# Full sections of 24 slots and three units' values, and one held bank for the value sums, in a fused Fourier-mix and attention kernel

## The chip, the cores and the metric

The kernel runs on one core of a Trainium2 chip. The metric is the device time of one execution in microseconds (us), as the median of several runs. The engines are PE (TensorE: matmuls; PEld is its weight loads), DVE (VectorE), ACT (ScalarE), POOL (GpSimd) and SP, which here only issues DMAs. PE writes its results into PSUM, which has eight banks of 128 x 512 floats; DVE and ACT read them from there.

## What is computed

The reference, cut to what matters (S = 2048 rows, D = 512, 32 heads of 16):

```python
g = sigmoid((x * gate_w).sum(-1, keepdims=True))
a = x @ dft_hid_re.T                 # DFT along the hidden axis
b = x @ dft_hid_im.T
y = dft_seq_re @ a - dft_seq_im @ b  # DFT along the sequence, real part
q, k, v = heads(x @ wqkv)
p = softmax(q @ k.T * 16 ** -0.5)    # 32 heads, 2048 x 2048
o = merge(p @ v) @ wo
out = g * y + (1 - g) * o
```

## The kernel before, in words

**Units.** Attention works on 16 pairs of heads. A pair is cut into 32 units: two halves of the queries (1024 each) times 16 tiles of 128 keys. A unit has four score products (two blocks of 512 queries, two heads), each a product of 64 rows with a 128 x 512 result, whose exponential ACT writes into a tile `pt`. Softmax needs the maximum of every query row first, so a second set of products ("maxima", L258) computes the scores the other way round some 70 tiles ahead, and DVE reduces each of those 128 x 512 tiles (L260). So a unit also needs four maxima products. The exact sums of the float32 DFT and projections are made of three products of rounded parts each (`ch`/`cl` are the two parts of a chunk of the DFT matrix).

**Sections.** PE's order is written out by patterns of slots. A slot of a section issues one product of a DFT or projection chain (L473) on one half of the 128 rows, and beside it one score (`s`, L797) or maxima (`a`, L258) product on the other half; the two run side by side. A section ends with `|`: there the planned loads are issued, and then the values of two units, products of `pt` with `vt` (L833), which use all 128 rows and 32 columns each, four beside each other. Sections come in pairs: the same chain products run first with rows 0 to 63 (half 0; the scores are those of head 1), then with rows 64 to 127 (half 1; the scores are those of head 0). Head 0 starts two units ahead, so that each section can end with the values of two units of both heads.

**Stages.** After the first projections, 12 pairs of THIN sections carry the real part of the hidden DFT, 96 pairs of FULL sections the DFT along the sequence, one EVEN and 15 TEN pairs the output projection; the last 16 units have a tail of their own. A FULL section has 16 slots, 8 of each kind. A chunk of the DFT matrix is 12 products; POOL splits it into two parts (`c_split`, L418 and L419) three chunks ahead, and SP loads it four chunks ahead (`c_load`). A whole sum over the sequence takes four chunks, 48 products; then ACT copies it out scaled (L527, L530).

**Banks.** One of the eight banks, `psD`, belongs to the chain. The other seven are handed out by `bank()`, a small planner that keeps for each bank the time at which it expects its reader to be done, and takes the one that comes free first. Which bank a product gets is thereby fixed when the program is built. Scores and maxima take banks, and so did each section's values: `pv` took one, ACT copied it to `oe` (L842), and POOL added it to `osum` (L848) in the next section. The first copy of each sixteen units goes straight to `osum` (L839).

**Order between halves.** The first chain product of a section waits for a reader of the section before: the exponential of its last score product (`tc.add_manual_dep` in `segment`).

**Buffers.** `pt` has four buffers of four 512-column blocks, one per unit. A buffer is handed out again when all that read it are done; the first exponential into it waits for that.

Of the kernel before, what the change touches and what calls it, by code (L numbers as in the profile page):

```python
# [13 lines left out]
ALU = mybir.AluOpType  # L14
# [18 lines left out]
def mix_kernel(ctx: ExitStack, tc: tile.TileContext, xa_t, xa, wqkv, w_hid, w_seq, wo, gate_w, out):  # L33
# [487 lines left out]
    def dft_next(c, tt, s, t, chain, yr):  # L521
        if c == 0 and tt == NT - 1:
            nc.sync.dma_start(t.bitcast(F32), b_d[s])
        if s == NT - 1:
            y = work.tile([P, D], F32, name="y", bufs=2)
            if c == 0:
                nc.scalar.activation(y, chain.ps, AF.Copy, scale=g[:, tt:tt + 1])  # L527
# [12 lines left out]
        if s % 4 == 3:  # L540
            i = (c * NT + tt) * 4 + s // 4
            c_split(i + 3)
            c_load(i + 4)


# [110 lines left out]
    def finish(ps, t, y, other=False, n=1):  # L656
        if other:

            for c in range(n):
                cols = slice(c * D // n, (c + 1) * D // n)  # L660
                tmp = few[0][:, t % 4, cols]
# [104 lines left out]
    last_pairs = []  # L766

    def last_pair(fill):
        few.append(work.tile([P, 4, D], F32, name="few", tag="pt", bufs=4))
# [13 lines left out]
    def scores(u, qb, h, ps=None):  # L783
        p, r = divmod(u, 32)
        hf, kt = divmod(r, 16)
        q0 = hf * 1024 + qb * 512
        if u >= UNITS - 16:

            blk, kt = divmod(kt, 8)
            q0, kt = 1024 + blk * 512, 2 * kt + qb  # L790
        if u not in pts:
            pts[u] = work.tile([P, 4, 512], F32, name="pt", bufs=4)
        if ps is None:
            i, ps = bank()
            read_by(i, "s")
        rr = slice(64 * h, 64 * h + 64)
        nc.tensor.matmul(ps, ks[p % 2][rr, kt * P:(kt + 1) * P], qs[p % 2][rr, q0:q0 + 512], start=True, stop=True)  # L797
        return nc.scalar.activation(pts[u][:, 2 * qb + h], ps, AF.Exp, bias=0.0, scale=DH ** -0.5)  # L798

    held = []  # L800

    def pv_last(u):
        nonlocal now
        blk, k2 = divmod(u - UNITS + 16, 8)
        pt = pts.pop(u)
        if k2 == 0:
            i, acc = bank()
            free[i] = 1e9
            held[:] = [i]
            last_pairs.append(LastPair(blk, acc))  # L810
        acc = last_pairs[-1].acc
        for j in range(4):
            x, h = divmod(j, 2)
            nc.tensor.matmul(acc[32 * j:32 * j + 32], vt[:, 2 * k2 + x, NP - 1, h:h + 32], pt[:, j],  # L814
                             start=k2 == 0, stop=k2 == 7)
        now += 3.75
        if blk == 0 and k2 == 7:
            last_pairs[0].copy(1)
            free[held[0]] = now + 6

    osum = work.tile([P, 2, 512], F32, name="osum", tag="w15")

    def pv(us):

        nonlocal now
        i, acc = bank()
        for u in us:
            p, r = divmod(u, 32)
            hf, kt = divmod(r, 16)
            pt = pts.pop(u)  # L830
            for j in range(4):
                h = j % 2
                nc.tensor.matmul(acc[32 * j:32 * j + 32], vt[:, kt, p, h:h + 32], pt[:, j],  # L833
                                 start=u == us[0], stop=u == us[-1])
        now += 3.75 * len(us) + 1
        read_by(i, "s")
        o = osum[:, hf]
        if kt + 1 == len(us):
            nc.scalar.copy(o, acc)  # L839
            return  # L840
        oe = work.tile([P, 512], F32, name="oe", bufs=2)
        nc.scalar.copy(oe, acc)  # L842
        adds.append(partial(add_sum, o, oe, p, hf, kt == NT - 1))

    adds = []

    def add_sum(o, oe, p, hf, whole):
        nc.gpsimd.tensor_tensor(o, o, oe, ALU.add)  # L848
        if whole:
            for qb in range(2):  # L850
                nc.sync.dma_start(o_d[hf][p, :, qb * 512:(qb + 1) * 512], o[64 * qb:64 * qb + 64])

    def add_sums():
        while adds:
            adds.pop(0)()

    def take(gen, n, whole=True):

# [37 lines left out]
    for p in range(2, NP):  # L896
        u = 32 * (p - 1)
        at(u - 18, load_q, p, LOW)
        for kb in range(4):
            cols = slice(kb * 512, (kb + 1) * 512)  # L900
            if 2 < p < NP - 1:
                at(u - 16 + 4 * kb, load_rows, p, 1, cols, (1,))
                at(u - 14 + 4 * kb, load_rows, p, 1, cols, (0,))
            else:
                at(u - 14 + 4 * kb, load_rows, p, 1, cols)
        at(u - 2, load_q, p, HIGH)

    for hf in range(2):
# [28 lines left out]

    FULL = "a s a s a s a s s a s a s a a s |"  # L940
    THIN = "aS s a s a s s a s a s a a sA |"
    EVEN = "aA s s a s ^ s d s sA a d sS |", "a s a sS a ^ s a s s s s a |"
    TEN = "aA s s a s ^ s s s a a sS |", "a s a sS a ^ s s s s s aA |"
# [19 lines left out]
            else:  # L963
                users.append((kind, scores(*x)))

    def values():
        nonlocal valued
        us = valued, valued + 1
        valued += 2
        if us[0] < UNITS - 16:  # L970
            pv(us)
        else:
            for u in us:
                pv_last(u)

    def segment(pattern, half, ds, stop, between=None, hold=True):


        nonlocal now
        nonlocal users  # L980
        before, users = users, []
        ds, late = iter(ds), []
        back = late if hold else None
        for n, slot in enumerate(pattern.split()):
            if slot == "|":
                for f in late:
                    f()
                add_sums()
                run_plan(valued)
                if between:  # L990
                    between()
                values()
                continue
            if slot == "^":
                if deferred:
                    deferred.pop(0)()
                continue
            now += 1
            ahead = n and len(slot) == 1 and slot != "d" and pattern in (THIN, *TEN)
            if ahead:  # L1000
                score(slot[0], 1 - half)
            if len(slot) == 1:
                x = next(ds, None)
                if x:

                    before = before if x[0].begun else None
                    i = issue(x, half, stop, back)
                    users = []
                    if before:
                        tc.add_manual_dep(  # L1010
                            i.ins, dict(before[::-1]).get("s", before[0][1]).ins.name,
                            mybir.DependencyInfo(mybir.DependencyClass.Sync, mybir.DependencyReason.DATA))
                        before = None
            if not ahead and slot != "d":
                score(slot[0], 1 - half)
            if len(slot) == 2:
                score(slot[1].lower(), half)
        if deferred:
            deferred.pop(0)()

    def pairs():

        for i in range(NT - 4):
            yield (THIN,) * 2, take(hid, 12)
        for i in range(2 * NT * 3):
            yield (FULL,) * 2, take(seq, 16)
        for patterns, n in ((EVEN, 1), (TEN, 15)):
            for i in range(n):
                yield patterns, take(both_first, 9)
# [14 lines left out]
    def first_tiles(phase, j):  # L1044
# [16 lines left out]
    def in_between():  # L1061
# [49 lines left out]
```

## Time and profile before

| | |
|---|---|
| time, median of 3 runs | 1651.18 us (1650.62 to 1653.74) |
| profiled execution, first to last instruction | 1649.2 us |
| PE busy | 1641.4 us, clock granted in full |
| DVE busy | 1356.8 us |
| ACT busy | 1268.2 us |
| POOL busy | 754.5 us |

The page gives no time of its own for the profiled execution beside its span; the runs were timed apart from it. In the profile's rows, `L473` is a line of the kernel, `d<-xab,ch` the tile written and those read, `x16` a number of instructions, and in a timeline the first two columns are the start and the length in us. A bracket at the end is idle time before the instruction and what ended it. In the rows by group, the numbers behind the bar are the busy time in us, the mean length of one in ns, and the idle time ahead with what ended most of it. In the rows by window, the busy time of PE, PEld, DVE, ACT and POOL follow the window's length, and the granted clock stands before the share of the DMA engines. A value product of float32 is recorded as two matmuls.

### The profile page before, as it was taken

The numbers are of one execution on the slowest core, as the hardware profiler recorded it, in microseconds if no ns is written. First come the engines' busy times: TensorE is split into PE (matmuls) and PEld (weight loads), VectorE is DVE, ScalarE is ACT, GpSimd is POOL, SyncE is SP. The second block draws the span as 40 slices with busy tenths as digits, with TensorE's granted clock in tenths as the row PEclk, the third lists the DMA queues.
The fourth block names the chain that finished last, engine by engine and source line by source line (L and its number), as shares of the span: only waits on it lengthen the run. The fifth ranks groups of instructions, "written<-read, shape, count | busy, mean of one in ns | idle before, by whom it ended". The sixth has DMA issues, their size and how long they took to land.

```text
span 1649.2 us, 35245 instructions
## 1 busy us (share of the span) xinstructions
PE 1641.4 (100%) x13169; PEld 1017.0 (62%) x13169; DVE 1356.8 (82%) x2285; ACT 1268.2 (77%) x2487; POOL 754.5 (46%) x813
## 2 busy tenths in 40 slices
PE   9999999999999999999999999999999999999998
PEld 7888855556656666566665666666666556655544
DVE  5469988888888888888888888888888888877776
ACT  5312188888888888888888888887888888899996
POOL 0224643554544555545454565554545566332341
PEclk9999999999999999999999999999999999999999
DMA  9953301112221224222227334322222233451024
GB/s 291 353 161 135 155 14 38 29 53 66 67 72 52 62 86 134 74 62 70 57 75 258 86 94 116 96 77 68 66 72 74 81 111 107 156 195 45 15 53 143
DMA packets 93346, 165.67 MB, mean 100 GB/s; under 512 B 23456, under 2 KB 26408, under 8 KB 92024
## 3 DMA queue, kind: packets, MB, share of 16 engines
q1 hardware_dynamic: 88536, 162.64, 31.9%
q8 instruction: 104, 1.70, 0.4%
q0 software_dynamic: 4352, 0.39, 0.2%
q14 instruction: 66, 0.54, 0.1%
q10 hardware_dynamic: 288, 0.39, 0.1%
HBM read 107.73 MB, written 54.52 MB: 98 GB/s over the span
## 4 chain that ended last, share of the span: by engine, by line
PE 99%; DMA 0%; DVE 0%; ACT 0%; DVEq 0%; SPq 0%; issue 0%
PE d L473 46%; PE t L833 28%; PE t L258 6%; PE t L797 6%; PE t L354 5%; PE t L92 2%; PE t L91 2%; PE t L93 2%; PE t L814 1%; PE t L473 1%; PE t L378 1%; PE t L192 0%; DMA raw<-wqkv 0%; DVE yp L665 0%; PE t L751 0%; PE t L729 0%
## 5 line engine op out<-in xcount | busy, mean ns | idle before, releaser
L260 DVE TENSOR_REDUCE mx<-t 128x1 f32<-128x512 f32 x2008 | 1232.8, 684 | 223.1 <-PE t L258 205.4
L798 ACT ACTIVATE pt<-t 128x512 f32<-128x512 f32 x2048 | 1031.1, 626 | 14.9 <-PE t L797 3.2
L258 PE MATMUL t<-ks,qs 64*128 64x512 f32 x2008 | 748.4, 406 | 0.0
L797 PE MATMUL t<-qs,ks 64*128 64x512 f32 x2048 | 729.4, 394 | 0.2
L473 PE MATMUL d<-xab,ch 64*128 64x512 f32 x2016 | 644.6, 394 | 0.0
L833 PE MATMUL t<-pt,vt 128*32 128x512 f32 x3968 | 477.1, 598 | 0.0
L473 PEld LDWEIGHTS d<-xab,ch 64*128 64x128 f32 x2016 | 366.7, 184 | 168.6 <-issue 67.1
L473 PE MATMUL d<-xab,cl 64*128 64x512 f32 x1008 | 397.7, 395 | 0.0
L258 PEld LDWEIGHTS t<-ks,qs 64*128 64x128 f32 x2008 | 355.9, 184 | 50.4 <-ACT pt L798 24.5
L797 PEld LDWEIGHTS t<-qs,ks 64*128 64x128 f32 x2048 | 368.5, 184 | 28.2 <-DVE mx L260 7.4
L848 POOL TENSOR_TENSOR osum<-osum,oe 128x512 f32<-128x512 f32 x217 | 279.7, 1289 | 157.4 <-ACT oe L842 155.3
L842 ACT COPY oe<-t 128x512 f32<-128x512 f32 x217 | 127.5, 588 | 182.3 <-PE t L833 175.2
L473 PEld LDWEIGHTS d<-xab,cl 64*128 64x128 f32 x1008 | 185.6, 184 | 85.8 <-issue 41.9
L833 PEld LDWEIGHTS t<-pt,vt 128*32 128x32 f32 x3968 | 103.6, 109 | 217.8 <-issue 149.1
L418 POOL CAST ch<-craw 128x512 fp32r<-128x512 f32 x126 | 77.4, 614 | 339.7 <-PE t L258 227.4
L419 POOL TENSOR_TENSOR cl<-craw,ch 128x512 fp32r<-128x512 f32 x126 | 162.5, 1289 | 10.2
L281 POOL DMA_DIRECT2D qs<-mt x132 | 73.8, 565 | 80.9 <-DVE mt L277 71.3
L473 PE MATMUL d<-wo_hl,o_hl 64*128 64x512 f32 x288 | 77.8, 402 | 0.0
L473 PE MATMUL d<-wre,xab 64*128 64x512 f32 x288 | 72.2, 394 | 0.0
L473 PEld LDWEIGHTS d<-wo_hl,o_hl 64*128 64x128 f32 x288 | 49.5, 184 | 15.9 <-ACT pt L798 13.4
L473 PEld LDWEIGHTS d<-wre,xab 64*128 64x128 f32 x288 | 50.9, 184 | 0.9
L91 PE MATMUL t<-xab,wh 128*128 128x512 f32 x120 | 46.7, 389 | 0.0
(123 smaller groups left out, 938.8 us busy)
## 6 DMA issues: line engine op xcount, KB each, us to landing
craw<-w_seq SPq DMA_DIRECT2D x128, 256.0 KB
qk<-hl SPq DMA_DIRECT2D x32, 512.0 KB
qs<-qk SPq DMA_DIRECT2D x84, 128.0 KB
ks<-qk SPq DMA_DIRECT2D x288, 32.0 KB
b<-hl SPq DMA_DIRECT2D x16, 512.0 KB
xab<-b SPq DMA_DIRECT2D x16, 512.0 KB
o<-osum SPq DMA_DIRECT2D x62, 128.0 KB
oh<-nh SPq DMA_DIRECT2D x12, 512.0 KB
```

Source lines behind the costliest of these rows:

```text
L91: nc.tensor.matmul(ps, sh, mh, start=first, stop=False)
L258: nc.tensor.matmul(ps, qs[p % 2][r, qt * P:(qt + 1) * P], ks[p % 2][r, kb * 512:(kb + 1) * 512], start=True, stop=True)
L260: user = nc.vector.tensor_reduce(mx[p % 2][:, h, qt, kb:kb + 1], ps, AX.X, ALU.max)
L354: i = nc.tensor.matmul(ps[c], st[r], mv[r], start=phase < 2 and j == 0, stop=phase > 1 and j == 11)
L418: nc.gpsimd.tensor_copy(h1, raw)
L419: nc.gpsimd.tensor_tensor(l1, raw, h1.bitcast(F32), ALU.subtract)
L473: i = nc.tensor.matmul(self.ps, st[r], mv[r], start=not self.begun, stop=stop)
L797: nc.tensor.matmul(ps, ks[p % 2][rr, kt * P:(kt + 1) * P], qs[p % 2][rr, q0:q0 + 512], start=True, stop=True)
L798: return nc.scalar.activation(pts[u][:, 2 * qb + h], ps, AF.Exp, bias=0.0, scale=DH ** -0.5)
L833: nc.tensor.matmul(acc[32 * j:32 * j + 32], vt[:, kt, p, h:h + 32], pt[:, j], start=u == us[0], stop=u == us[-1])
L842: nc.scalar.copy(oe, acc)
L848: nc.gpsimd.tensor_tensor(o, o, oe, ALU.add)
```

## The change

FULL sections get 24 slots and the values of three units, so that the 384 units of that stage take 64 pairs in place of 96. Head 0 starts three units ahead. `pt` becomes eight buffers of two blocks, one per unit and head. The value sums of sixteen units stay in one bank, which `pv` takes with the first of them and ACT copies to `osum` after the last; the copies to `oe` and the adds on POOL go. The split that follows an even chunk is issued at the section's end. The rows of the keys are loaded for both heads at once.

```diff
@@ dft_next
-            c_split(i + 3)
+            if i % 2:
+                c_split(i + 3)
+            else:
+                at(valued + 1, c_split, i + 3)
             c_load(i + 4)
@@ scores
-        if u not in pts:
-            pts[u] = work.tile([P, 4, 512], F32, name="pt", bufs=4)
+        if (u, h) not in pts:
+            pts[u, h] = work.tile([P, 2, 512], F32, name="pt", bufs=8)
...
-        return nc.scalar.activation(pts[u][:, 2 * qb + h], ps, AF.Exp, bias=0.0, scale=DH ** -0.5)
+        return nc.scalar.activation(pts[u, h][:, qb], ps, AF.Exp, bias=0.0, scale=DH ** -0.5)
@@ pv
-    def pv(us):
+    accs = []
+
+    def pv(u):
         nonlocal now
-        i, acc = bank()
-        for u in us:
-            p, r = divmod(u, 32)
-            hf, kt = divmod(r, 16)
-            pt = pts.pop(u)
-            for j in range(4):
-                h = j % 2
-                nc.tensor.matmul(acc[32 * j:32 * j + 32], vt[:, kt, p, h:h + 32], pt[:, j],
-                                 start=u == us[0], stop=u == us[-1])
-        now += 3.75 * len(us) + 1
-        read_by(i, "s")
-        o = osum[:, hf]
-        if kt + 1 == len(us):
-            nc.scalar.copy(o, acc)
-            return
-        oe = work.tile([P, 512], F32, name="oe", bufs=2)
-        nc.scalar.copy(oe, acc)
-        adds.append(partial(add_sum, o, oe, p, hf, kt == NT - 1))
+        p, r = divmod(u, 32)
+        hf, kt = divmod(r, 16)
+        if kt == 0:
+            accs[:] = bank()
+            free[accs[0]] = 1e9
+        i, acc = accs
+        pt = [pts.pop((u, h)) for h in range(2)]
+        for j in range(4):
+            x, h = divmod(j, 2)
+            nc.tensor.matmul(acc[32 * j:32 * j + 32], vt[:, kt, p, h:h + 32], pt[h][:, x], start=kt == 0, stop=kt == NT - 1)
+        now += 3.75
+        if kt == NT - 1:
+            read_by(i, "s")
+            nc.scalar.copy(osum[:, hf], acc)
+            stores.append(partial(store_sum, p, hf))
@@ plan of the loads
-            if 2 < p < NP - 1:
-                at(u - 16 + 4 * kb, load_rows, p, 1, cols, (1,))
-                at(u - 14 + 4 * kb, load_rows, p, 1, cols, (0,))
-            else:
-                at(u - 14 + 4 * kb, load_rows, p, 1, cols)
+            at(u - 14 + 4 * kb, load_rows, p, 1, cols)
@@ patterns
-    FULL = "a s a s a s a s s a s a s a a s |"
+    FULL = "a s a s a s a s a s a s s a s a s a s a s a a s |"
@@ pairs
-        for i in range(2 * NT * 3):
-            yield (FULL,) * 2, take(seq, 16)
+        for i in range(2 * NT * 2):
+            yield (FULL,) * 2, take(seq, 24)
@@ first_tiles
+        if j == 6 and phase in (1, 2):
+            scores(*next(streams[0][0]), turn_of("a"))
@@ the loop over the sections
-            segment(patterns[half], half, ds, half == 1)
+            segment(patterns[half], half, ds, half == 1, n_values=3 if patterns[0] is FULL else 2)
```

What moves on PE, at the end of a section in the middle of the FULL stage. Before (`t` is a bank of the seven, `d` the chain's):

```order
L473 MATMUL d<-xab_178,ch 128x512
L797 MATMUL t<-qs_940,ks_941 128x512
L833 MATMUL t<-pt,vt 32x512 x8
L473 MATMUL d<-xab_177,ch 128x512
L258 MATMUL t<-ks_939,qs_938 128x512
```

The same place now (the score product's line is L800, the values' L840):

```order
L258 MATMUL t<-ks_939,qs_938 128x512
L473 MATMUL d<-xab_180,cl 128x512
L800 MATMUL t<-qs_940,ks_941 128x512
L840 MATMUL t<-pt,vt 32x512 x12
L473 MATMUL d<-xab_177,ch 128x512
```

Twelve value products stand together where there were eight, after 24 pairs of products in place of 16, and the bank that they write stays the same over sixteen units.

On ACT, over the end of a FULL section; the numbers tell tiles apart, and in brackets stand the engines waited for. Before:

```order
L798 ACTIVATE pt_12565<-t_12566 128x512 [waits PE_49,Activation_49]
L798 ACTIVATE pt_12565<-t_12579 128x512 [waits PE_49]
L842 COPY oe_12592<-t_12583 128x512 [waits PE_49,Pool_49]
L798 ACTIVATE pt_12547<-t_12602 128x512 [waits PE_49]
L798 ACTIVATE pt_12547<-t_12610 128x512 [waits PE_49]
```

Now:

```order
L801 ACTIVATE pt_12734<-t_12743 128x512 [waits PE_49]
L801 ACTIVATE pt_12751<-t_12752 128x512 [waits PE_49,Activation_49]
L801 ACTIVATE pt_12751<-t_12770 128x512
L801 ACTIVATE pt_12800<-t_12801 128x512 [waits PE_49]
L801 ACTIVATE pt_12800<-t_12809 128x512 [waits PE_49]
```

The copy between the sections is gone. The eleventh exponential of a section (the first into `pt_12751`) waits for a value product that stands on PE behind the twelfth score product, since the ninth live `pt` takes the buffer of the oldest; the twelfth needs no wait of its own behind it.

More of the change, by code (lines that the diff above doesn't have):

```diff
@@ L660, in finish @@
                 cols = slice(c * D // n, (c + 1) * D // n)
-                tmp = few[0][:, t % 4, cols]
+                tmp = few[0][:, t % 4 // 2, cols]
                 nc.scalar.activation(tmp, ps[:, cols], AF.Copy, scale=omg[:, t:t + 1])
@@ L768, in last_pair @@
     def last_pair(fill):
-        few.append(work.tile([P, 4, D], F32, name="few", tag="pt", bufs=4))
+        few.append(work.tile([P, 2, D], F32, name="few", tag="pt", bufs=8))
         x = last_pairs[1]
@@ L813, in pv_last @@
             x, h = divmod(j, 2)
-            nc.tensor.matmul(acc[32 * j:32 * j + 32], vt[:, 2 * k2 + x, NP - 1, h:h + 32], pt[:, j],
+            nc.tensor.matmul(acc[32 * j:32 * j + 32], vt[:, 2 * k2 + x, NP - 1, h:h + 32], pt[h][:, x],
                              start=k2 == 0, stop=k2 == 7)
@@ L821, in mix_kernel, with store_sum @@
     osum = work.tile([P, 2, 512], F32, name="osum", tag="w15")
-    def pv(us):
+    accs = []
+    def pv(u):
         nonlocal now
-        i, acc = bank()
-        for u in us:
-            p, r = divmod(u, 32)
-            hf, kt = divmod(r, 16)
-            pt = pts.pop(u)
-            for j in range(4):
-                h = j % 2
-                nc.tensor.matmul(acc[32 * j:32 * j + 32], vt[:, kt, p, h:h + 32], pt[:, j],
-                                 start=u == us[0], stop=u == us[-1])
-        now += 3.75 * len(us) + 1
-        read_by(i, "s")
-        o = osum[:, hf]
-        if kt + 1 == len(us):
-            nc.scalar.copy(o, acc)
-            return
-        oe = work.tile([P, 512], F32, name="oe", bufs=2)
-        nc.scalar.copy(oe, acc)
-        adds.append(partial(add_sum, o, oe, p, hf, kt == NT - 1))
[L845 to L855, printed above, removed]
+        p, r = divmod(u, 32)
[4 more added lines that the diff above has]
+        i, acc = accs
+        pt = [pts.pop((u, h)) for h in range(2)]
+        for j in range(4):
[6 more added lines that the diff above has]
+            stores.append(partial(store_sum, p, hf))
+    stores = []
+    def store_sum(p, hf):
+        for qb in range(2):
+            nc.sync.dma_start(o_d[hf][p, :, qb * 512:(qb + 1) * 512], osum[64 * qb:64 * qb + 64, hf])
     def take(gen, n, whole=True):
@@ L964, in score, with values, segment @@
                 users.append((kind, scores(*x)))
[L966 to L976, printed above, removed]
+    def values(n):
+        nonlocal valued, now
+        for u in range(valued, valued + n):
+            (pv if u < UNITS - 16 else pv_last)(u)
+        valued += n
+        now += 1
+    def segment(pattern, half, ds, stop, between=None, hold=True, n_values=2):
         nonlocal now
@@ L987, in segment @@
                     f()
-                add_sums()
+                while stores:
+                    stores.pop(0)()
                 run_plan(valued)
@@ L991, in segment @@
                     between()
-                values()
+                values(n_values)
                 continue
```

## The prediction, made before the changed kernel was run

> **What bounds the kernel now.** I read the page first, then the windows view by stage, then the timeline of single sections, because the page's averages hide what ends last inside a section.
>
> ```profile
> span 1649.2 us, 35245 instructions
> PE 1641.4 (100%) x13169; PEld 1017.0 (62%) x13169; DVE 1356.8 (82%) x2285; ACT 1268.2 (77%) x2487; POOL 754.5 (46%) x813
> PEclk9999999999999999999999999999999999999999
> 217.00:345.20 128.20, 128.20 (x1016) 70.07 (x1012) 112.89 (x190) 109.60 (x219) 56.67 (x64) 1.00 0.10 28
> 345.20:1446.50 1101.30, 1101.30 (x9222) 671.07 (x9218) 944.56 (x1590) 909.81 (x1772) 565.17 (x606) 1.00 0.31 90
> 1446.50:1600.00 153.50, 153.50 (x1222) 79.10 (x1220) 115.73 (x189) 147.27 (x288) 50.50 (x51) 1.00 0.23 76
> ```
>
> PE is never without a matmul and its clock is full, so the time is PE's pace. The windows are the THIN stage, the FULL stage (two thirds of the time) and EVEN/TEN. FULL has 192 sections (96 pairs), so one takes 1101.3/192 = 5.736 us; DVE is 86% busy there and ACT 83%: close behind PE. One FULL section, where the first column is the start, the second the length:
>
> ```profile
> 804.04 0.49 PE L473 MATMUL d<-xab,ch 64*128 64x512 f32 x1
> ...
> 804.23 0.59 ACT L842 COPY oe<-t 128x512 f32<-128x512 f32 x1 [1.07 <-PE t L833]
> 804.37 0.39 PE L473 MATMUL d<-xab,cl 64*128 64x512 f32 x1
> ...
> 804.58 4.88 DVE L260 TENSOR_REDUCE mx<-t 128x1 f32<-128x512 f32 x8 [0.83 <-PE t L258]
> 804.61 0.39 PE L473 MATMUL d<-xab,ch 64*128 64x512 f32 x1
> ...
> 804.84 4.03 ACT L798 ACTIVATE pt<-t 128x512 f32<-128x512 f32 x8
> ...
> 807.60 0.39 PE L797 MATMUL t<-qs,ks 64*128 64x512 f32 x1
> 807.92 1.92 PE L833 MATMUL t<-pt,vt 128*32 128x512 f32 x16
> ...
> 808.38 0.13 PEld L833 LDWEIGHTS t<-pt,vt 128*32 128x32 f32 x4 [0.30 <-issue]
> 808.80 0.13 PEld L833 LDWEIGHTS t<-pt,vt 128*32 128x32 f32 x4 [0.30 <-issue]
> 809.77 0.50 PE L473 MATMUL d<-xab,ch 64*128 64x512 f32 x1
> ```
>
> I count from the section's first product (804.04 = 0). Sixteen slots, each a DFT product beside a scores or maxima product on the other half of the rows, start from 0 to 3.56 (807.60), 0.23 apart once running (804.37, 804.61). After 0.32 the values begin, and 1.85 after that the next section (809.77). The value loads are 0.43 apart, so four groups cost 1.72, a unit 0.86. What is left over, 5.736 - 16 x 0.23 - 1.72 = 0.34, is the price of one change to the value shape and back.
>
> The second reading is the drain. Each slot fills a PSUM bank that DVE or ACT must read.
>
> ```profile
> L260 DVE TENSOR_REDUCE mx<-t 128x1 f32<-128x512 f32 x2008 | 1232.8, 684 | 223.1 <-PE t L258 205.4
> L798 ACT ACTIVATE pt<-t 128x512 f32<-128x512 f32 x2048 | 1031.1, 626 | 14.9 <-PE t L797 3.2
> ```
>
> Eight maxima without a gap take 4.88 and one takes 0.684, so they start (4.88 - 0.684)/7 = 0.60 apart; eight exponentials likewise (4.03 - 0.626)/7 = 0.486. Together that is one bank per 1/(1/0.60 + 1/0.486) = 0.268 us, while PE fills one per 0.23. PE outruns its readers in every section; the banks store the difference and the values let them empty. With seven banks it just works: when slot 16 comes, at 3.56, nine of the fifteen tiles before it must have been read. Maximum k ends at 0.54 + 0.60(k - 1) + 0.684 and exponential k at 0.80 + 0.486(k - 1) + 0.626: four maxima by 3.02, five exponentials by 3.37. The margin is 0.19 us.
>
> **The change, part by part.**
>
> *Fewer sections.* FULL becomes 128 sections of 24 slots and three units. Unhindered, the 24th slot starts at 3.56 + 8 x 0.23 = 5.40, and the section ends 0.32 + 1.85 + 0.86 later: 8.43. 128 x 8.43 = 1079.0, against 1101.3: **-22.3 us**.
>
> *One bank fewer, FULL.* The sum now holds its bank for sixteen units, so six remain for slots. The 24th slot needs 18 of the 23 tiles before it read. The pattern alternates, and the program makes it wait for the eighth maximum and the tenth exponential: 0.54 + 7 x 0.60 + 0.684 = 5.42 and 0.80 + 9 x 0.486 + 0.626 = 5.80, and these are the earliest times, with neither engine ever idle. What a waiting product costs on top is shown in the THIN stage:
>
> ```profile
> 228.06 0.50 PE L258 MATMUL t<-ks,qs 64*128 64x512 f32 x1
> ...
> 228.68 4.03 ACT L798 ACTIVATE pt<-t 128x512 f32<-128x512 f32 x8
> 231.29 0.18 PEld L258 LDWEIGHTS t<-ks,qs 64*128 64x128 f32 x1
> 231.30 0.50 PE L258 MATMUL t<-ks,qs 64*128 64x512 f32 x1
> 231.73 1.92 PE L833 MATMUL t<-pt,vt 128*32 128x512 f32 x16
> ```
>
> The product at 231.30 waits for the fifth exponential (228.68 + 4 x 0.486 + 0.626 = 231.25). Its weights are loaded only 0.04 later, and it lasts 0.50 instead of 0.39 because of that: 0.05 + 0.10 in all. So the 24th product streams at 5.80 + 0.15 = 5.95 instead of 5.40: 0.55 us lost. Earlier slots of the section wait too, within this total. 128 x 0.55 = **+70.4 us**. Bounds: 0.45 if no load is exposed, 0.65 if the ACT pace slips by 0.01 over ten exponentials: 58 to 83.
>
> The Trainium skill (TensorE: Matmul & The Clock Gate, "Part 3: Packing small matmuls — row/col tiling") says that PE pulls a weight load ahead of matmuls still running when it goes to other rows. By it the 0.10 would be hidden, and this term be an estimated 128 x 0.45 = 58 us. The row at 231.29 speaks against it for a load that has to wait.
>
> *The same bank, THIN.* The section's last maxima product waits for the sixth exponential in place of the fifth: 0.486 later. The copy no longer stands ahead of the first exponential, which may start up to 0.04 earlier. 24 sections x 0.45 = **+10.8 us**.
>
> *The same bank, EVEN and TEN.* Two neighbouring sections:
>
> ```profile
> 1480.90 4.03 ACT L798 ACTIVATE pt<-t 128x512 f32<-128x512 f32 x8
> ...
> 1483.07 1.93 PE L833 MATMUL t<-pt,vt 128*32 128x512 f32 x16
> ...
> 1485.68 4.03 ACT L798 ACTIVATE pt<-t 128x512 f32<-128x512 f32 x8
> ...
> 1487.81 1.92 PE L833 MATMUL t<-pt,vt 128*32 128x512 f32 x16
> ```
>
> The fourth exponential ends at 1480.90 + 3 x 0.486 + 0.626 = 1482.98 and at 1487.76. Now the values themselves wait for it, and start 0.09 and 0.05 later. After the change the last product waits for it, starts 0.05 later, and the values follow that product by 0.43 (as 231.73 follows 231.30): 1483.46 and 1488.24, later by 0.39 and 0.43. 32 x 0.41 = **+13.1 us**.
>
> *Buffers by head.* In FULL nine half buffers would be alive and there are eight, so the eleventh exponential writes one that the first unit's values must have read; ACT and its twelfth queue behind. Values start at V; that unit's two groups end at V + 0.46 + 0.60 (the groups' rows):
>
> ```profile
> L833 PE MATMUL t<-pt,vt 128*32 128x512 f32 x3968 | 477.1, 598 | 0.0
> L842 ACT COPY oe<-t 128x512 f32<-128x512 f32 x217 | 127.5, 588 | 182.3 <-PE t L833 175.2
> L848 POOL TENSOR_TENSOR osum<-osum,oe 128x512 f32<-128x512 f32 x217 | 279.7, 1289 | 157.4 <-ACT oe L842 155.3
> L527 ACT ACTIVATE y<-d,g 128x512 f32<-128x512 f32 x16 | 12.2, 760 | 0.0
> L418 POOL CAST ch<-craw 128x512 fp32r<-128x512 f32 x126 | 77.4, 614 | 339.7 <-PE t L258 227.4
> L419 POOL TENSOR_TENSOR cl<-craw,ch 128x512 fp32r<-128x512 f32 x126 | 162.5, 1289 | 10.2
> ```
>
> With 0.12 until ACT starts (estimated from the copy at 804.23), the two exponentials run from V + 1.18 to V + 2.30. The next section's first DFT product waits for the twelfth, and would start at V + 2.71 anyway: hidden, 0.36 spare. But every fourth section ends a DFT chain, whose scaled copy (L527, and its twin L530) stands behind them: V + 2.16 + 0.76 = 2.92, the product streams at 3.07 instead of 2.81. 32 x 0.26 = **+8.3 us**, 0 at best.
>
> *The rest, at nothing.* The 217 copies (0.588) and adds (1.289) were on ACT and POOL, which PE did not wait for beyond what is counted. Key rows for both heads in one go mean fewer DMA issues; loads are planned ten units or more ahead. The even chunk's split moves from its slot to the section's end: POOL then does two splits of 0.614 + 1.289 = 1.9 us in a row, done about 4.3 after the last slot starts (two splits and 0.5 for that slot's product), and the first product that reads the later one is slot 13 of the next section, some 6 us after the last slot (3.0 of values, 12 slots). The load issued between them waits on SP for about 4 us with stores and row loads behind it, which have tens of us. If that cover were gone, the 64 splits would cost up to 2 us each.
>
> Sum: -22.3 + 70.4 + 10.8 + 13.1 + 8.3 = **+80.3 us** on the span of 1649.2. The median of the runs, 1651.18, is 2.0 above that span; I keep that distance: 1731.5. Bounds of the terms: +68 - 8 - 4 = +56 to about +100, so 1707 to 1751 for this case alone.
>
> **The rivals.**
>
> *The switch is what counts (faster).* Slots keep their 0.23 and only the 64 dropped switches remain: 1651.2 - 22.3 = **1629**. It decides at 0.17: if the 24th product waits less than 22.3/128 = 0.17 us, FULL gains. For it: 0.34 per switch is really there, and no FULL section waits on a bank today. Against: 18 tiles would have to be read by 5.42 (5.57 less 0.15), and the readers, never idle, need until 5.80. The skill's TensorEngine Tiling (Array Packing), "Key Properties", that changing the tiling mode drains the engine, would give this result; no row of it counts banks.
>
> *The bank bites half as much.* Banks come free unevenly, and a late bank is partly hidden by the DFT product that still runs beside. Half of 94.3: -22 + 47 + 8 = +33, **1684**. Against: in the THIN row the wait is seen whole.
>
> *ACT closes the circle (slower still).* The held-back exponentials have 0.36 us spare in each section. If ACT runs 0.3 later than reckoned, every fourth section loses that and the others begin to: 128 x 0.2 = 26 more, **1757**. Against: ACT has 12 exponentials, 5.8 us, in a section of nearly 9.
>
> **How the numbers follow.** The forecast 0.74, the faster rival 0.08, half 0.11, slower still 0.07. The predicted time is 1731.5. The range is 1684 to 1760: the half case's centre up to just past the ACT case, which leaves out the faster rival, the lower half of the half case and the forecast's tails. About 0.2% (3.3 us) is what a measurement of this kernel tells from no change: faster 0.09, same 0.02, slower 0.89.
>
> **What would show it.** Right: 128 FULL sections near 9.0 us instead of 8.43; the last slots of each spaced by 0.27 to 0.45 instead of 0.23, with weight-load waits on maxima and exponentials; THIN near 6.0, TEN near 5.2; DVE idle over 1.5 us between sections. Wrong: slots at an even 0.23 to the 24th and FULL near 1079 us (the faster rival); or first DFT products that wait on exponentials in every section (the ACT case). If FULL is as computed and the other stages do not move, the bank count is right but the place of the wait in the short sections is not.

## The result and the profile after

After the change a run takes 1940.1 us in the median (1938.3 to 1940.5), before it 1650.9: a ratio of 1.175, with a 95% interval of 1.173 to 1.177. The forecast was 1731.5, with a range up to 1760. The sign was right, the size was not: 289 us were lost where 80 were forecast.

The page of the kernel after, its first lines and the clock's:

```profile
span 1936.5 us, 34137 instructions
PE 1776.9 (92%) x13169; PEld 1056.1 (55%) x13169; DVE 1365.7 (71%) x2285; ACT 1165.2 (60%) x2270; POOL 474.0 (24%) x596
PEclk9999999999998989999998988999989898999999
```

PE executes as many matmuls as before but now stands for 8% of the span, and its clock is no longer granted in full everywhere. The windows by stage, THIN, FULL and EVEN/TEN, in the columns explained above:

```profile
217.40:353.46 136.06, 136.06 (x1016) 68.74 (x1013) 112.81 (x190) 99.31 (x198) 33.08 (x46) 1.00 0.09 27
353.46:1722.39 1368.93, 1217.14 (x9221) 712.70 (x9217) 952.99 (x1590) 832.30 (x1604) 346.84 (x436) 0.94 0.23 73
1722.39:1887.60 165.21, 165.16 (x1222) 77.16 (x1218) 115.96 (x189) 131.84 (x261) 13.30 (x22) 1.00 0.20 64
```

Against before's 128.20, 1101.30 and 153.50, THIN lost 7.9 us (forecast 10.8) and EVEN/TEN 11.7 (forecast 13.1). FULL lost 267.6, of which PE stood for 1368.93 - 1217.14 = 151.8. For FULL the forecast had 56.

The sections of half 1 are as reckoned. One of them, from its first product to the next section's:

```profile
814.53 0.49 PE L473 MATMUL d<-xab,ch 64*128 64x512 f32 x1
...
815.36 5.01 ACT L801 ACTIVATE pt<-t 128x512 f32<-128x512 f32 x10 [1.28 <-PE t L800]
...
818.83 0.50 PE L258 MATMUL t<-ks,qs 64*128 64x512 f32 x1
...
819.44 0.49 PE L258 MATMUL t<-ks,qs 64*128 64x512 f32 x1
...
820.51 0.41 PE L800 MATMUL t<-qs,ks 64*128 64x512 f32 x1
...
820.84 2.78 PE L840 MATMUL t<-pt,vt 128*32 128x512 f32 x24
...
823.56 0.50 PE L473 MATMUL d<-xab,ch 64*128 64x512 f32 x1
```

The section takes 9.03 us (8.98 forecast). The 24th slot starts 5.98 after the first (5.95 forecast), the last eight slots are 0.23 to 0.34 apart, and the two maxima products shown, which waited for a bank, last 0.50 and 0.49.

The sections of half 0 are not. A row of their own shows it in the view of PE's waits; the columns are the wait in all, how often, and the longest. Before the change the view has one row alone:

```profile
PE t L162 <- DVE zero L60: 1.1, 1, 1.1
```

Now its longest rows are these:

```profile
PE t L258 <- DMA ks<-qk: 118.8, 30, 8.3
PE d L473 <- POOL ch L418: 8.7, 14, 0.8
```

Maxima products wait for key rows, in 30 sections. The timeline of one of these:

```profile
407.55 0.61 POOL L418 CAST ch<-craw 128x512 fp32r<-128x512 f32 x1
408.24 1.29 POOL L419 TENSOR_TENSOR cl<-craw,ch 128x512 fp32r<-128x512 f32 x1
...
409.56 0.33 SPq L408 DMA_DIRECT2D craw<-w_seq  x1
409.70 0.39 PE L473 MATMUL d<-xab,ch 64*128 64x512 f32 x1
409.99 1.77 SPq L230 DMA_DIRECT2D ks<-qk  x3
...
413.54 0.46 PE L258 MATMUL t<-ks,qs 64*128 64x512 f32 x1 [3.45 <-DMA ks<-qk]
...
415.59 0.62 PE L800 MATMUL t<-qs,ks 64*128 64x512 f32 x1
...
418.42 0.39 PE L800 MATMUL t<-qs,ks 64*128 64x512 f32 x1
```

POOL ends the postponed split at 409.53. At 409.56 SP can issue the chunk load (L408) that had waited for it, and only then the key rows (L230), which take 1.77 us to issue; the last of them was issued at 411.76, and PE goes on at 413.54. The rows were wanted by the fifth slot, at 409.70. The section took 13.98 us. After it a product takes 0.62 instead of 0.39 for a while, because the stall also costs clock (last section).

### The profile page after: what moved, and what is told of

It is laid out like the page before. It is cut to its first block, busy times and chain, and to the rows that moved or that the text cites. A ratio compares the mean times of both kernels' runs of the same rounds, so it can differ in the third digit from the quotient of the medians.

```text
span 1936.5 us, 34137 instructions
## 1 busy us (share of the span) xinstructions
PE 1776.9 (92%) x13169; PEld 1056.1 (55%) x13169; DVE 1365.7 (71%) x2285; ACT 1165.2 (60%) x2270; POOL 474.0 (24%) x596
## 4 chain that ended last, share of the span: by engine, by line
PE 80%; POOL 5%; issue 5%; DMA 4%; ACT 3%; SPq 2%; DVE 1%; DVEq 0%; POOLq 0%; ACTq 0%
PE t L840 20%; PE t L258 17%; PE d L473 17%; PE t L800 15%; PE t L354 5%; DMA ks<-qk 3%; POOL cl L419 2%; ACT pt L801 2%; SPq L230 1%; PE t L93 1%; PE t L91 1%; PE t L92 1%; POOL ch L418 1%; DVE mx L260 1%; PE t L817 1%
## 5 line engine op out<-in xcount | busy, mean ns | idle before, releaser
L801 ACT ACTIVATE pt<-t 128x512 f32<-128x512 f32 x2048 | 1054.5, 618 | 597.9 <-PE t L840 223.6
L258 PE MATMUL t<-ks,qs 64*128 64x512 f32 x2007 | 832.3, 441 | 127.4 <-DMA ks<-qk 118.8
L800 PE MATMUL t<-qs,ks 64*128 64x512 f32 x2048 | 794.7, 419 | 7.1 <-ACT pt L801 7.0
L473 PE MATMUL d<-xab,ch 64*128 64x512 f32 x2016 | 688.9, 422 | 12.1 <-POOL ch L418 8.7
L258 PEld LDWEIGHTS t<-ks,qs 64*128 64x128 f32 x2007 | 368.8, 193 | 298.1 <-issue 130.6
L840 PE MATMUL t<-pt,vt 128*32 128x512 f32 x3968 | 465.6, 599 | 0.0
L473 PEld LDWEIGHTS d<-xab,ch 64*128 64x128 f32 x2016 | 380.0, 196 | 141.3 <-ACT pt L801 78.8
L800 PEld LDWEIGHTS t<-qs,ks 64*128 64x128 f32 x2048 | 387.2, 194 | 104.3 <-ACT pt L801 52.7
L473 PE MATMUL d<-xab,cl 64*128 64x512 f32 x1008 | 431.4, 428 | 5.3 <-POOL cl L419 5.3
L840 PEld LDWEIGHTS t<-pt,vt 128*32 128x32 f32 x3968 | 110.4, 110 | 237.1 <-issue 228.6
L531 POOL TENSOR_TENSOR y<-y,yr 128x512 f32<-128x512 f32 x16 | 20.6, 1287 | 208.9 <-ACT y L530 208.9
L91 PE MATMUL t<-xab,wh 128*128 128x512 f32 x120 | 46.7, 389 | 0.0
L92 PE MATMUL t<-xab,wh 128*128 128x512 f32 x120 | 46.7, 389 | 0.0
```

Source lines behind the costliest of these rows:

```text
L91: nc.tensor.matmul(ps, sh, mh, start=first, stop=False)
L92: nc.tensor.matmul(ps, sh, ml, start=False, stop=False)
L258: nc.tensor.matmul(ps, qs[p % 2][r, qt * P:(qt + 1) * P], ks[p % 2][r, kb * 512:(kb + 1) * 512], start=True, stop=True)
L473: i = nc.tensor.matmul(self.ps, st[r], mv[r], start=not self.begun, stop=stop)
L801: return nc.scalar.activation(pts[u, h][:, qb], ps, AF.Exp, bias=0.0, scale=DH ** -0.5)
```

## The experiments

Three theories stood against each other. A: the key rows are asked for too late by the plan, since the maxima run ahead in bursts of six units. B: they are asked for in time, but stand in SP's queue behind the chunk load that waits for the postponed split. C: the splits on POOL are themselves late. In the table "FULL" is that stage's length in the profiled execution, "PE" the time in it that PE was busy; both are from the windows view. Each ratio is against runs of the kernel before on the same chip. That kernel took 1653.6 beside the four experiments down to "before, one held bank" and 1650.6 to 1650.9 beside the rest, so a difference between the two groups is good to about 3 us.

| kernel | time, us | ratio to before (95%) | FULL | PE |
|---|---|---|---|---|
| before | 1650.9 | 1 | 1101.3 | 1101.3 |
| after | 1940.1 | 1.175 (1.173 to 1.177) | 1368.9 | 1217.1 |
| split at once | 1770.0 | 1.070 (1.069 to 1.072) | 1200.2 | 1166.8 |
| chunk behind rows | 1784.7 | 1.079 (1.078 to 1.081) | 1218.0 | 1174.5 |
| rows by head | 1813.7 | 1.097 (1.095 to 1.098) | 1242.9 | 1182.6 |
| before, one held bank | 1708.2 | 1.033 (1.031 to 1.034) | 1138.9 | 1138.9 |
| rows at once | 1761.6 | 1.067 (1.066 to 1.069) | 1191.5 | 1166.7 |
| seven banks | 1724.8 | 1.044 (1.043 to 1.046) | 1174.5 | 1140.2 |
| nine buffers | 1748.1 | 1.059 (1.058 to 1.061) | 1179.1 | 1166.3 |
| steps apart | 1743.9 | 1.057 (1.055 to 1.058) | 1174.8 | 1161.7 |
| seven banks, steps apart | 1701.5 | 1.030 (1.029 to 1.032) | 1149.8 | 1130.2 |
| nine buffers, steps apart | 1738.0 | 1.053 (1.051 to 1.054) | 1165.1 | 1159.7 |

**Split at once.** The changed kernel, with the split in its slot again:

```diff
-            if i % 2:
-                c_split(i + 3)
-            else:
-                at(valued + 1, c_split, i + 3)
+            c_split(i + 3)
             c_load(i + 4)
```

> The changed kernel with one edit taken back: the split of the chunk that follows an even chunk is issued in its slot again, not at the section's end. In the changed kernel the load of the next chunk, which follows it in SP's queue, waits for that split, and the key rows asked for at the section's end stand behind the load. Theory A (the merged key rows are asked for too late by the plan, whatever stands in the queue): the long half-0 sections stay, 1890 us or more. Theory B (the rows stand behind the load that waits for the postponed split): the queue is free at the section's end; rows are needed 3.0 us of values and 13 or 4 slots of 0.23 later, 6.0 or 3.9 us, and take 1.8 us to issue and 1.75 to land, so nearly all of the 207 us of surplus goes: 1940 - 207 + at most 25 = 1733 to 1760 us. Theory C (POOL's two splits in a row are themselves late): the same time as B here.

It ran in 1770.0: 170 of the 208.6 us beyond the forecast go with this edit. Theory A falls as the main cause. The range of B and C ended 10 us lower, and the reason is in a section that is still long:

```profile
687.93 0.33 SPq L528 DMA_DIRECT2D yr<-y  x1
...
688.36 0.38 SPq L408 DMA_DIRECT2D craw<-w_seq  x1
688.79 0.56 SPq L598 DMA_DIRECT2D no<-o  x1
...
692.25 1.81 SPq L230 DMA_DIRECT2D ks<-qk  x3
...
696.04 0.76 PE L258 MATMUL t<-ks,qs 64*128 64x512 f32 x1 [4.41 <-DMA ks<-qk]
```

The rows stand behind the store of the chain's scaled copy and four loads that the planner puts at the same section end. It is the same queue with other things in it.

**Chunk behind rows.** The split stays postponed; only the order in SP's queue changes:

```diff
             if i % 2:
                 c_split(i + 3)
+                at(valued + 1, c_load, i + 4)
             else:
                 at(valued + 1, c_split, i + 3)
-            c_load(i + 4)
+                c_load(i + 4)
```

> The changed kernel with the postponed split left where it is, but the chunk load that waits for it put behind the key rows in SP's queue. Theory B (queue order alone): the rows go out at the section's end and the surplus goes, but the splits stay late, which cost about 1.4 us in a dozen sections: 1740 to 1760 us. Theory A (rows asked for too late): no change, 1890 us or more. Theory C (POOL's splits are late): no change, 1900 us or more.

1784.7: the order alone gives back 155 us, so B holds. It missed its range by 25, and the waits of PE in this kernel say what C is worth:

```profile
PE d L473 <- POOL ch L418: 9.6, 14, 1.2
PE t L258 <- DMA ks<-qk: 9.4, 5, 3.3
PE d L473 <- POOL cl L419: 9.0, 15, 0.6
```

So C is true of some 15 sections, 18.6 us. They are in the second half of FULL, where POOL also adds the real part (L531, 1.29 us) between a chain's end and the postponed split. With the split at once there is no such wait.

**Rows by head.** Each head's key rows are asked for at the end of the section that scored the old ones last:

```diff
-            at(u - 14 + 4 * kb, load_rows, p, 1, cols)
+            if p == 2:
+                at(u - 14 + 4 * kb, load_rows, p, 1, cols)
...
+    def rows_after(u, qb, h):
+        p, r = divmod(u, 32)
+        if 0 < p < NP - 2 and r > 15 and r % 4 == 3 and qb:
+            kb = r % 16 // 4
+            rows_due.append(partial(load_rows, p + 2, 1, slice(kb * 512, (kb + 1) * 512), (h,)))
...
                 users.append((kind, scores(*x)))
+                rows_after(*x)
...
+                while rows_due:
+                    rows_due.pop(0)()
                 run_plan(valued)
```

> The changed kernel with the key rows loaded for each head by itself, at the end of the section in which the last score product on the rows that they replace was issued; split and chunk load as in the changed kernel. As in the changed kernel, head 1's maxima over one block of keys in three are issued before the load and read the rows of the pair two before. Theory A: most of the surplus of 207 us goes, 1733 to 1770 us. Theory B: the rows of head 1 now go out one section earlier, between a half-0 and a half-1 section, where no chunk load waits; they are early in spite of the queue, so also 1740 to 1780 us: this run does not tell A from B, but says whether earlier rows are a cure by themselves.

1813.7, outside both ranges, though better by 126 us. PE hardly waits for key rows any more. What I had left out is that the query rows, and the clearing of one of them (L235), stand in the same queue. The longest row of PE's waits in this kernel:

```profile
PE t L258 <- DMA qs<-zero: 23.9, 8, 4.6
```

One in three of the requests for a half of the query rows has its first use, by head 1's maxima, in the section right behind it. So asking earlier cures the key rows, and the blocked queue finds its next customer. Head 1's key rows now go out at a section's end where no chunk load waits, so this run does not tell A from B.

**Before, one held bank.** The kernel before with `pv` keeping one bank for sixteen units (the new `pv`, `store_sum` and `accs` of the change with the old layout of `pt`); nothing else.

> The kernel before with one edit of the change: the value sums of sixteen units stay in one bank, so that six are left for slots; sections of 16 slots and two units, buffers, splits and key rows as before. The forecast's reckoning of the bank, by itself: THIN +8 to +11, EVEN and TEN +12 to +13, and in FULL the 16th slot waits for the fifth maximum (3.62 + 0.15 = 3.77 against 3.56) or, if a sixth exponential is needed, until 3.86 + 0.15 = 4.01: 192 x 0.21 to 0.45 = 40 to 86 us. Together 1711 to 1761 us. Rival (the copies and adds that go with it free ACT and POOL enough to pay for the bank): 1651 us or less.

1708.2, 3 us below the range. The windows:

```profile
217.00:353.05 136.05, 136.05 (x1016) 68.77 (x1012) 112.81 (x190) 99.30 (x198) 33.02 (x46) 1.00 0.10 26
353.05:1491.93 1138.88, 1138.88 (x9221) 694.79 (x9217) 943.88 (x1590) 811.19 (x1604) 352.72 (x437) 1.00 0.29 87
1491.93:1655.70 163.77, 163.77 (x1220) 77.22 (x1216) 115.92 (x189) 131.16 (x260) 12.81 (x22) 1.00 0.22 70
```

THIN loses 7.8 us, FULL 37.6 (0.196 a section, for the 0.21 of a wait for the fifth maximum), EVEN/TEN 10.3. ACT is busy some 125 us less and POOL 275, and nothing of that comes back: the bank was the scarce thing, not the engines.

**Rows at once.** Split at once, and each head's rows asked for right behind the last score product on the old ones, ahead of the section's end:

```diff
                 rows_after(*x)
+                while rows_due:
+                    rows_due.pop(0)()
```

> The changed kernel with the split in its slot again, as in the first experiment, and the key rows of each head asked for right behind the last score product on the rows that they replace, ahead of the section's end and so ahead of what the planner issues there. If the queue is the whole cause, what the first experiment left over in long half-0 sections (42 us above 9.05 a section, half of it seen as maxima waiting for key rows behind a store of the scaled copy and the planner's loads) goes by 25 to 35 us: 1735 to 1745 us, and FULL near the forecast's 1101.3 - 22.3 + 70.4 + 8.3 = 1158 us. If what is left is a fault of the shorter lead itself, which issuing earlier by a part of a section does not mend: 1760 to 1770 us.

1761.6: 8 us, not 25 to 35. That lies in the range of the other case, but a lead too short is only part of what is left: it sits mostly in five sections (13.9 to 14.9 us instead of 9), and in three of these PE waits for ACT, not for key rows. One of the three starts at 1008.8; the timeline of POOL, ACT and PE:

```profile
1008.76 1.29 POOL L531 TENSOR_TENSOR y<-y,yr 128x512 f32<-128x512 f32 x1 [4.39 <-ACT y L530]
...
1009.99 0.62 POOL L418 CAST ch<-craw 128x512 fp32r<-128x512 f32 x1
...
1011.91 1.26 POOL L613 TENSOR_TENSOR no<-no 128x512 f32<-128x512 f32 x1
1013.20 0.62 ACT L87 CAST nh<-no 128x512 fp32r<-128x512 f32 x1 [4.51 <-POOL no L613]
...
1014.37 0.79 PE L803 MATMUL t<-qs,ks 64*128 64x512 f32 x1 [3.48 <-ACT pt L804]
```

Two planned steps of a block of the output projection, due two units apart, fall into one section end: ACT's cast, issued ahead of the section's exponentials, waits for POOL's product, and the exponentials queue behind the cast.

**Seven banks.** Rows at once, but with a bank for each section's values, copied by ACT and added by POOL as before (two banks where sixteen units end inside a section). The edit of `values`; that `pv` again takes a bank for each sum and uses `oe` is not shown:

```diff
-        for u in range(valued, valued + n):
-            (pv if u < UNITS - 16 else pv_last)(u)
...
+        cut = next((k for k in range(1, n) if us[k] % 16 == 0), n)
+        pv(us[:cut])
+        if cut < n:
+            pv(us[cut:])
```

> The same kernel as the one with rows at once, but without the held bank: sections of 24 slots and three units stay, and each section's value sum takes a bank of its own that ACT copies out and POOL adds, as before the change (two banks where a sum of sixteen units ends inside a section). Forecast's reckoning: the bank's price goes, THIN and EVEN/TEN come back to before's times (-20 us), and in FULL the values start at the tenth exponential, 5.80 + 0.15, where the 24th slot did, so a section is 0.32 to 0.43 shorter than 9.0: 128 x 0.37 = -47 us against the held bank. So 65 to 70 us below the one with rows at once, 1668 to 1680 us: fewer sections alone do not beat the kernel before. Rival (the dropped switches are worth 0.34 each once the bank is back): 1629 to 1645 us.

1724.8, some 45 us above the range. Part of it is stalls of the two kinds above, 34 us of standing. The rest is taken up in "Seven banks, steps apart", where fewer of them are left.

**Nine buffers.** Rows at once with `bufs=9` for `pt`; the copy of the last sums moves into one of them.

> The same kernel as the one with rows at once, with nine half buffers for the exponentials instead of eight (the copy of the last sums moves into one of them), so that the eleventh exponential does not wait for the first unit's values. Forecast: only the sections behind the end of a chain gain, 32 x 0.18 to 0.26 = 6 to 8 us less. Rival (ACT's circle is what holds the sections, the bank only shows it): 128 x 0.2 to 0.4 = 26 to 51 us less. If the two exponentials are hidden everywhere: no difference.

13.6 us less, where 6 to 8 were forecast. In FULL that is 12.4: the sections at whose end a chain ends go from about 9.3 to 9.03, as forecast, and the long ones get shorter, which was not. Most other sections stay near 9.03, so ACT's circle is not what holds them, and that rival falls.

**Steps apart.** Rows at once with one number changed, so that no two steps of a block meet:

```diff
-                    for step, du in enumerate((16, 20, 22)):
+                    for step, du in enumerate((16, 19, 22)):
```

> The kernel with rows at once and eight half buffers, with one number changed: the three planned steps of a block of the output projection's operand (load, product on POOL, rounding on ACT) are due 16, 19 and 22 units behind instead of 16, 20 and 22. In sections of three units the second and the third step fell into the same section end in four cases, so ACT's rounding, issued ahead of the next exponentials, waits for POOL's product, which stands behind the splits. Theory (a plan made for steps of two units): the three long sections near the 261st, 285th and 405th unit, 5 us too long each, go, and the key rows that stood behind the block's store come up to 9 us sooner: 1738 to 1747 us. Rival (the splits on POOL are late whatever the plan): 1760 us.

1743.9, in the range. The three long sections in which PE waited for ACT are gone; two of 15.1 us remain, in which it waits for key rows for 2.9 and 3.3 us. PE's longest waits in this kernel are now

```profile
PE t L258 <- DMA ks<-qk: 6.7, 3, 3.3
PE d L473 <- ACT y L530: 3.0, 15, 0.2
```

FULL is 1174.8 with PE busy 1161.7; the forecast's terms for it (-22.3, +70.4, +8.3 on 1101.3) make 1157.7. With most of the stalls out, the forecast's sum for FULL is 4 us short of PE's busy time; whether its terms are right is taken up below.

**Seven banks, steps apart.** The same number in the kernel with seven banks.

> The same single number in the kernel with 24 slots and seven banks, whose nine long sections hold 37 us: 21 to 35 us less, 1690 to 1704 us. Its FULL sections then stand at 8.78 us without surplus, 128 x 8.78 = 1124 us, against 1101 for the 192 shorter ones of the kernel before: if that holds, longer sections lose without the held bank too. Rival (the dropped switches pay once nothing else stalls): 1651 us or less.

1701.5, in the range, and still 51 us above the kernel before. FULL's window, and one undisturbed section of it:

```profile
346.11:1495.95 1149.84, 1130.16 (x9220) 696.62 (x9216) 938.65 (x1590) 886.35 (x1724) 503.15 (x557) 1.00 0.29 87
```

```profile
853.10 0.50 PE L473 MATMUL d<-xab,ch 64*128 64x512 f32 x1
...
853.94 5.00 ACT L804 ACTIVATE pt<-t 128x512 f32<-128x512 f32 x10
...
858.01 0.18 PEld L803 LDWEIGHTS t<-qs,ks 64*128 64x128 f32 x1 [0.25 <-ACT pt L804]
858.02 0.49 PE L803 MATMUL t<-qs,ks 64*128 64x512 f32 x1
...
858.85 0.39 PE L803 MATMUL t<-qs,ks 64*128 64x512 f32 x1
...
859.16 0.16 PEld L839 LDWEIGHTS t<-pt,vt 128*32 128x32 f32 x8 [0.36 <-ACT pt L804]
859.16 2.78 PE L839 MATMUL t<-pt,vt 128*32 128x512 f32 x24
...
861.87 0.50 PE L473 MATMUL d<-xab,ch 64*128 64x512 f32 x1
```

With seven banks the 24th slot starts 5.75 after the first, not 5.40, since slots before it wait for banks; the score product at 858.02 waits for an exponential. The values follow the 24th slot by 0.31, as before the change. They do not wait for the tenth exponential, as this run's expectation had it: that one had ended 0.22 earlier (853.94 + 5.00 = 858.94). The section takes 8.77 us. Three units in the short sections take 1.5 x 5.736 = 8.60. So 24 slots are slower than 16 even without the held bank: the switch saved is paid back to the readers. The kernel still has eight half buffers; seven banks with nine were not run.

**Nine buffers, steps apart.** Everything found, in one kernel: split and rows at once, nine buffers, steps apart.

> The same single number in the kernel with rows at once and nine half buffers, whose eight long sections hold 23 us: 10 to 20 us less, 1728 to 1738 us. This is the change with every stall taken out that was found; what remains above the kernel before is the bank and the longer sections.

1738.0, at the upper edge. 87 us above the kernel before remain with PE busy all but 5 us of FULL. No version of the change beat the kernel before. FULL makes 63.8 of the 87 us, 58.4 of them with PE busy; by the runs with one held bank and with seven banks this is mostly the price of late banks inside the sections.

## Why the prediction was wrong

**What held.** The 24th slot waits for the tenth exponential at the place and time reckoned (5.98 for 5.95; the exponential ends at 815.36 + 5.01 = 820.37, and the product follows 0.14 later, for 0.15), and THIN and EVEN/TEN came within 3 us of their terms. The change without most of its stalls (steps apart) takes 1743.9, 12.4 above the forecast, and PE still stands for 13.1 us of its FULL stage.

**The step that failed** is in "The rest, at nothing": "The load issued between them waits on SP for about 4 us with stores and row loads behind it, which have tens of us." I had the wait, its length and the queue right, and took the cover from the plan's "ten units or more ahead". The cover was not there. The planner's units count values; maxima of head 1 run far ahead of them, and in sections of three units they come in bursts of twelve, so a block of key rows planned 14 units ahead has its first use in slot 5, 14 or 22 of a half-0 section. The request stands at the end of the section ahead, 3.0 us of values and 4 or 13 slots earlier, 3.9 or 6.0 us; issuing takes 1.77 and landing 1.75. That leaves 0.4 to 2.5 us, and the queue takes about 4 (in the section shown 3.6, from the start of the values at 405.95 to 409.56). (Where the first use is slot 22, the request comes behind it in the program's order: those maxima read the rows of the pair two before, which changes the shift of the softmax's exponent and costs no wait.) Before the change head 1's rows were asked for two units earlier, with a whole section of half 1 and 13 slots in between. In the changed kernel PE waits for key rows for 118.8 us, in 30 sections, where the prediction had nothing.

The sentence that followed, "the 64 splits would cost up to 2 us each", had the right trigger and a price that was too low, and its 128 us stood neither in the sum nor in the range. A rival "the rows come late" at 128 us would have stood at 1860. It would still have been short, by the clock among other things: of the 211 us by which FULL exceeds the forecast's 1157.7, PE stood for 151.8, and it was busy 1217.1 - 1161.7 = 55 us more than in the kernel with most of the stalls out.

**Shares.** Of the 208.6 us beyond the forecast, 170.1 go with the split (155.4 come back by the queue's order alone), 8.4 with rows at once, 17.7 with the steps apart; 12.4 remain.

**A sum that was right for the wrong reason.** I put +70.4 to the bank and -22.3 to the fewer sections. With seven banks and 24 slots PE is busy 1130.2 in FULL, 28.9 more than before, not 22.3 less; the held bank adds 1161.7 - 1130.2 = 31.5, not 70.4. The two terms make 60.4 where I had 48.1, so that the sum came near is luck: one term was too small by 51 and the other too large by 39. Of the 28.9, about 21 show in the undisturbed section, 128 x (8.77 - 8.60); where the rest sits was not taken apart. The wait of the 24th slot was counted as the bank's, though most of it belongs to the longer section (5.40 to 5.75 with seven banks, 5.75 to 5.98 by the held one): readers take a bank every 0.268 us, PE fills one every 0.23, so each slot more in a row adds to what must wait. The faster rival (1629) fails for that reason, not for the bank alone.

**The copy's term.** +8.3 for the scaled copies behind the held-back exponentials: 9.75 us in FULL between the two kernels with steps apart, with eight and with nine buffers (1174.8 and 1165.1), some of it from long sections.

## What to carry to other kernels

A queue that one engine serves in order has no cover of its own: before a wait is put ahead of a load, take the load's first use in the program's order and the time from issue to landing, not the distance in the plan. When the step of a loop gets coarser, every due time that was set for the old step needs to be looked at again, since things that were apart now meet. And a longer run of one kind of work pays only while its readers keep pace; if they are slower, it saves switches and buys waits.

## What the hardware showed besides

A stall of PE can cost more than its length. The windows around the stall shown above, with the granted clock as the third number from the end:

```profile
410.10:413.54 3.44, 0.00 (x2) 0.04 (x2) 0.40 (x1) 0.45 (x1) 0.00 (x0) 1.00 0.50 155
413.54:414.70 1.16, 1.16 (x10) 1.14 (x12) 0.66 (x2) 0.37 (x1) 0.00 (x0) 1.00 0.74 205
414.70:418.20 3.50, 3.50 (x20) 3.30 (x19) 2.75 (x6) 2.98 (x6) 0.00 (x0) 0.51 0.67 173
```

After 3.44 us without a matmul PE runs 1.16 us at full clock; the 3.5 us behind that have a mean clock of 0.51. The Trainium skill (TensorE: Matmul & The Clock Gate, Part 1, on the HAM clock gate) has such a rule: half the clock after an idle window of about 3.4 us, full again after one that is busy, with windows that run free of the program. The trace agrees on the length: 0.51 over 3.5 us is some 3.4 us at half clock. The length of the stall needed does not quite agree, as the windows around a shorter stall show:

```profile
589.90:592.50 2.60, 0.05 (x2) 0.01 (x1) 0.88 (x2) 0.97 (x2) 0.00 (x0) 0.96 0.39 108
592.50:596.00 3.50, 3.48 (x18) 3.00 (x20) 2.21 (x4) 1.74 (x3) 0.00 (x0) 0.54 0.13 52
```

Here 2.6 us were enough, while the stall of 2.73 at 806.30 left the clock at 1.00. Windows that run free of the program can account for this. In the trace's clock records every stretch at half clock in FULL starts a whole number of 3.413 us steps from every other (414.78, 493.29, 592.27, 612.75). On that grid, PE was busy for 1.24 and 1.09 us of the windows that end where half clock starts, and for 1.70 us of the window that holds most of the stall at 806.30, behind which the clock stayed full:

```profile
411.37:414.78 3.41, 1.24 (x11) 1.25 (x12) 0.74 (x2) 0.45 (x1) 0.00 (x0) 1.00 0.58 162
588.86:592.27 3.41, 1.09 (x10) 0.48 (x6) 1.92 (x4) 2.01 (x5) 0.00 (x0) 1.00 0.38 107
807.31:810.73 3.42, 1.70 (x14) 1.55 (x16) 1.19 (x2) 0.96 (x2) 0.00 (x0) 1.00 0.36 108
```

So in this kernel a window need not be idle throughout: about two thirds of it were enough, and what a stall costs depends on where it falls on the grid.
